# Sharing the last product of a decode-attention kernel with GpSimd, with smaller last pieces behind it

## The chip, the core and the metric

The kernel runs on one core of a Trainium2 chip. Time is device time in microseconds (us), taken as the median of several executions; less is better. A core has TensorE (matrix products, PE in the rows), VectorE (DVE), ScalarE (ACT), GpSimd (POOL) and SyncE (SP, which here only issues loads). Each has its own instruction queue and they meet at semaphores. Sixteen DMA engines move data between HBM and the on-chip SBUF, whose 128 partitions are the rows of every tile; TensorE writes to PSUM.

## What is computed

One token for each of two sequences goes through cached attention with 16 heads, 4096 keys and a head size of 256, and through a small dense layer with a squared ReLU. A gate mixes the two.

```python
q = (x @ wq)                                   # 2 x 16 heads x 256
scores = einsum("bhqd,bhkd->bhqk", q, k_cache) * 256 ** -0.5
o = einsum("bhqk,bhkd->bhqd", softmax(scores), v_cache)
a = o.reshape(B, 1, 4096) @ wo
h = x @ w1 + b1;  b = relu(h) ** 2 @ w2 + b2
g = sigmoid((x * gate_w).sum(-1))
out = g * a + (1 - g) * b                      # 2 x 1 x 448, all float32
```

Each of the two caches has 134 MB, and with the weights 289.6 MB go through the core once.

## The kernel before

The two caches are read in 16 rounds. A round takes two heads `t` of one sequence `b`: 8 MB of keys and 8 MB of values. Keys and values lie with 64 of a head's 4096 keys in each partition (64 partitions for each of the two heads), so one partition holds 64 x 256 = 16384 numbers of each.

A round `r` runs through the engines like this:

- VectorE multiplies the whole key tile by q in place (line 213, the q of the head spread over 64 keys), which waits for the keys' landing; then it takes the reciprocal and the small product `rl` of the round before (`normed`, lines 198 and 199), sums each key's 256 products into `s` (line 222), and takes the maximum over the partition's 64 keys (`m`, line 223).
- TensorE spreads the maxima (`mt`), VectorE takes their maximum, negated (`nb`, line 224), ScalarE makes the exponentials `p` in two halves with their sums (line 240), and TensorE adds these sums over the partitions (`sm`).
- TensorE multiplies values by `p`: 32 matmuls into `po`, each written as two records in the profile since the numbers are float32. ScalarE copies `po` to `o` (line 193), TensorE turns it with `rl` as the scale (`ot`), and ScalarE copies the result into `oT` (line 194).

The loads stand in SyncE's queue in the order in which they are written, and each waits there for what frees its tile: keys of round r + 2 for the sums of round r, values of round r for TensorE's values of round r - 1. There are two key tiles and one value tile. The last values go into a free key tile instead, in two pieces cut at `V_CUT` keys, once the sums of round 14 are done. The output weights wo go into the value tile behind the values of round 14, in five pieces, cut after 16, 24, 28, 31 and 32 blocks (`WO_CUTS`).

After the last round comes the output projection: 32 blocks of 128 rows of wo. All but the last `LATE` are added into `acc`, with two rows of output and 448 columns; all matmul lines appear as line 265, a helper. The late ones are added into `fin`, 112 columns at a time in four parts of the array, from `wide`, into which VectorE has copied their part of `oT` (line 258). ScalarE copies `acc` to `ya` (line 260), and a matmul with `pick` adds it into `fin` in the middle of the late blocks. VectorE copies the result (`y`, line 261) and SyncE stores it.

```python
for i, (t, k) in enumerate(blocks):
    if i == WO_CUTS[i_w]:
        pe.wait_ge(WL[i_w].h, 16)
        i_w += 1
    ...
    if n == LATE // 2:
        pe.wait_ge(AC.h, AC_YA)
        late(pick, ya)
    ins = late(wide[:, n, :], rhs, n == 0, n == LATE - 1)
```

The name of a tile is given in the rows without its number: `k` is either key tile, `v` the value tile.

Of the kernel before, what the change touches and what calls it, by code (L numbers as in the profile page):

```python
# [7 lines left out]
ALU = mybir.AluOpType  # L8
AX = mybir.AxisListType

P = 128
WO_ORDER = [0, 1, 2, 3, 7, 4, 5, 6]
LATE = 8
WO_CUTS = (0, 16, 24, 28, 31, 32)
V_CUT = 48


class Count:
# [16 lines left out]
def gated_mix_kernel(nc, b2, wq, wf, wo, k_cache, v_cache, out):  # L35
    B, H, S, DH = k_cache.shape
# [5 lines left out]
    KEYS = 2 * S // P  # L42
# [11 lines left out]
    pe, dve, act, pool, sp = nc.tensor, nc.vector, nc.scalar, nc.gpsimd, nc.sync  # L54
    rounds = [(t, b) for t in range(T) for b in range(B)]
    R = len(rounds)

    def sb(name, *free):
        return nc.alloc_sbuf_tensor(name, [P, *free], F32)[:]
# [12 lines left out]
    pick = sb("pick", W)  # L72
    wide = sb("wide", LATE, W)
    p8 = sb("p", NM, 4)
    s = sb("s", KEYS)
# [18 lines left out]
    DV, AC, TE, GP = (Count(nc, n) for n in ("dve", "act", "pe", "pool"))  # L94
    KL = [Count(nc, "k0_landed"), Count(nc, "k1_landed")]
# [14 lines left out]
    def kv(cache, r):  # L110
        t, b = rounds[r]
        return cache[b, 2 * t:2 * t + 2].rearrange("h (p j) d -> (h p) (j d)", j=KEYS)

    def load(dst, src, sem, after=None):
        ins = sp.dma_start(dst, src)
        if after:
            after[0].on(ins, after[1])
        return sem.up(ins, 16)
# [10 lines left out]
    def te_mt(r):  # L129
        return TE_MT0 if r == 0 else TE_SUM0 + 4 * (r - 1) + 3  # L130
# [4 lines left out]
    def te_val(r):  # L135
        return TE_SUM0 + 4 * r + 1

    def te_ot(r):
        return TE_SUM0 + 4 * r + 2

    TE_ACC = te_ot(R - 1) + 1
    TE_FIN = TE_ACC + 1


    pool.memset(ident, 0.0)
    GP.up(pool.memset(ones, 1.0))
# [37 lines left out]
    AC_QB = [AC.up(TE.on(act.activation(qb[:, i, :], QBANK[i % 4], AF.Copy), TE_QB[i])) for i in range(T * B // 2)]  # L184
# [6 lines left out]
    def turned(r):  # L191
        t, b = rounds[r]
        OC.up(TE.on(act.activation(o, po, AF.Copy), te_val(r)))  # L193
        AC_OT[r] = AC.up(TE.on(act.activation(oT[:, t, :, b, :], ot[:, :NJ * 2].rearrange("p (j h) -> p j h", h=2), AF.Copy), te_ot(r)))  # L194

    def normed(r):
        b = rounds[r][1]
        n = DV.up(TE.on(dve.reciprocal(rc, sm[:, :2]), te_sum(r)))
        RL.up(DV.on(dve.scalar_tensor_tensor(rl, rc.unsqueeze(1).to_broadcast([P, 2, 2]), gP[:, 0, b:b + 1],
                                             sel.rearrange("p (s h) -> p s h", s=2), op0=ALU.mult, op1=ALU.mult), n))  # L200

    def k_view(r):
        return keys[r % 2].rearrange("p (j d) -> p j d", d=DH)

    load(keys[1], kv(k_cache, 1), KL[1], (TE, TE_Q1))
    for r, (t, b) in enumerate(rounds):
        kt = k_view(r)
        q = qb[:, (t // 2) * B + b, (t % 2) * DH:(t % 2 + 1) * DH]
        if r < 4:
            dve.wait_ge(AC.h, AC_QB[(t // 2) * B + b])  # L210
        elif r == 4:
            dve.wait_ge(AC.h, AC_QB[-1])
        n = DV.up(KL[r % 2].on(dve.tensor_tensor(kt, kt, q.unsqueeze(1).to_broadcast([P, KEYS, DH]), op=ALU.mult), 16 * (r // 2 + 1)))  # L213
        if r == 0:
            DV_H = DV.up(TE.on(dve.tensor_tensor(hb, sm[:, :FC * B].rearrange("p (c b) -> p c b", b=B), b1T.unsqueeze(2).to_broadcast([P, FC, B]), op=ALU.add), TE_PT))
            DV_H = DV.up(DV.on(dve.tensor_scalar(hb, hb, 0.0, None, op0=ALU.max), DV_H))
            DV_H = DV.up(DV.on(dve.tensor_mul(hT, hb, hb), DV_H))
            DV_H = DV.up(DV.on(dve.tensor_tensor(hT, hT, gP[:, 1, :].unsqueeze(1).to_broadcast([P, FC, B]), op=ALU.mult), DV_H))
            load(vals, kv(v_cache, 0), VL, (TE, TE_ADD))
        else:  # L220
            normed(r - 1)
        DV_S = DV.up(DV.on(dve.tensor_reduce(s, kt, axis=AX.X, op=ALU.add), n))  # L222
        MX.up(DV.on(dve.tensor_reduce(m, s, axis=AX.X, op=ALU.max), DV_S))
        DV_NB = DV.up(TE.on(dve.tensor_reduce(nb, mt[:, :64], axis=AX.X, op=ALU.max, negate=True), te_mt(r)))  # L224
        if r > 0:
            turned(r - 1)
            if r < R - 1:
                load(vals, kv(v_cache, r), VL, (TE, te_val(r - 1)))
            else:
                for i, (lo, hi) in enumerate(zip(WO_CUTS, WO_CUTS[1:])):  # L230
                    load(vals[:, lo * D:hi * D], wo[:, lo * D:hi * D], WL[i], (TE, te_val(r - 1)) if i == 0 else None)
        if r + 2 < R:
            load(keys[r % 2], kv(k_cache, r + 2), KL[r % 2], (DV, DV_S))
        elif r + 2 == R:
            at = V_CUT * DH
            load(keys[r % 2][:, :at], kv(v_cache, R - 1)[:, :at], VT[0], (DV, DV_S))
            load(keys[r % 2][:, at:], kv(v_cache, R - 1)[:, at:], VT[1])
        for hh in range(2):
            z = slice(64 * hh, 64 * hh + 64)
            e = act.activation(p8[z, :, hh:hh + 3:2], s[z].rearrange("p (m s) -> p m s", s=2), AF.Exp,  # L240
                               bias=nb[z], accum_out=rsm[z, hh:hh + 1])
            if hh == 0:
                DV.on(e, DV_NB)
            else:
                EX.up(e)
# [3 lines left out]
    blocks = [(t, k) for t in WO_ORDER for k in range(4)]  # L249
    early = len(blocks) - LATE  # L250

# [21 lines left out]
    def done(ins, n):  # L273
        ins.then_inc(TE.h, 1)
        te[0] += 1
        assert te[0] == n, (te[0], n)

    def values(v, lo=0, hi=NM):
        vv = v.rearrange("p (m s d) -> p m (s d)", s=2, d=DH)
        for i in range(lo, hi):  # L280
            g = 32 * (i % 4)
            ins = mm(po[g:g + 4, :], p8[:, i, :], vv[:, i, :], i < 4, i >= NM - 4)
        return ins

    def turn():
        take(OC)
        take(RL)
        for j in range(NJ):
            for x in range(2):
                at = x * DH + j * P  # L290
                ins = mm(ot[:, j * 2:j * 2 + 2], o[:, at:at + P], rl[:, x, :], x == 0, x == 1)
        return ins
# [11 lines left out]

    n_acc = 1 + FC + T * 4 - LATE
    added = [0]
# [7 lines left out]
    def late(lt, rhs, start=False, stop=False):  # L314
        for k in range(4):
            ins = mm(fin[32 * k:32 * k + W, :DQ], lt, rhs[:, k * DQ:(k + 1) * DQ], start, stop)
        return ins
# [59 lines left out]
    pe.wait_ge(VT[0].h, 16)  # L377
    values(keys[R % 2], 0, V_CUT // 2)
    pe.wait_ge(VT[1].h, 16)
    done(values(keys[R % 2], V_CUT // 2, NM), te_val(R - 1))  # L380
    done(turn(), te_ot(R - 1))
    pe.wait_ge(AC.h, AC_OT[R - 1])
    i_w = 0
    for i, (t, k) in enumerate(blocks):
# [9 lines left out]
        n = i - early  # L394
        if n == 0:
            pe.wait_ge(DV.h, DV_W)
# [4 lines that stand above are left out]
    done(ins, TE_FIN)  # L401
# [74 lines left out]
```

## Time and profile before

| what | value |
|---|---|
| median of 3 runs | 677.21 us (676.92 to 678.72) |
| the profiled execution's own time | 678.37 us |
| its span | 676.2 us |
| mean granted TensorE clock | 0.641 |
| VectorE busy | 566.5 us, 84% |
| TensorE busy | 219.1 us, 32% |
| GpSimd busy | 2.1 us, all in the first 3 us |
| moved by DMA | 289.63 MB, mean 428 GB/s |

The span goes from the first to the last recorded instruction of the execution; the execution's own time is 2.2 us longer. In the rows a group has its source line, its engine, the operation, the tile written and the tile read, with partitions x elements; a bracket at the end of a row tells how long the engine had been idle and which engine or transfer released it. The clock is the share of full speed that TensorE was granted.

### The profile page before, as it was taken

The numbers are of one execution on the slowest core, as the hardware profiler recorded it, in microseconds if no ns is written. First come the engines' busy times: TensorE is split into PE (matmuls) and PEld (weight loads), VectorE is DVE, ScalarE is ACT, GpSimd is POOL, SyncE is SP. The second block draws the span as 40 slices with busy tenths as digits, with TensorE's granted clock in tenths as the row PEclk, the third lists the DMA queues.
The fourth block names the chain that finished last, engine by engine and source line by source line (L and its number), as shares of the span: only waits on it lengthen the run. The fifth ranks groups of instructions, "written<-read, shape, count | busy, mean of one in ns | idle before, by whom it ended". The sixth has DMA issues, their size and how long they took to land. (4 is left out here: it accounts for less than half of the span.)

```text
span 676.2 us, 3474 instructions
## 1 busy us (share of the span) xinstructions
PE 219.1 (32%) x1522; PEld 68.1 (10%) x1522; DVE 566.5 (84%) x120; ACT 36.1 (5%) x111; POOL 2.1 (0%) x15
## 2 busy tenths in 40 slices
PE   0726142140605123060603206060512406050368
PEld 0211001010101101010100101010010101010022
DVE  1067999999979797998979798997979799897950
ACT  0121000000000000000000000000000000000000
POOL 1000000000000000000000000000000000000000
PEclk9976656585756557575755757575665758575568
DMA  9999999999999999999999999999999999999996
GB/s 381 438 445 421 434 435 434 434 434 434 434 435 434 430 434 431 434 434 434 434 434 434 434 434 434 434 434 434 434 434 434 434 434 434 434 434 434 418 423 284
DMA packets 5779, 289.63 MB, mean 428 GB/s; under 512 B 653, under 2 KB 782, under 8 KB 1038
## 3 DMA queue, kind: packets, MB, share of 16 engines
q1 hardware_dynamic: 5772, 289.56, 99.1%
q8 instruction: 3, 0.05, 0.0%
q14 instruction: 2, 0.02, 0.0%
q10 hardware_dynamic: 2, 0.00, 0.0%
HBM read 289.55 MB, written 0.00 MB: 428 GB/s over the span
## 5 line engine op out<-in xcount | busy, mean ns | idle before, releaser
L213 DVE TENSOR_TENSOR k<-k,q 128x16384 f32<-128x16384 f32 x16 | 275.6, 17224 | 52.7 <-DMA k<-in_k_cache_dram 52.7
L222 DVE TENSOR_REDUCE s<-k 128x64 f32<-128x16384 f32 x16 | 275.4, 17212 | 0.0
L265 PE MATMUL po<-v,p 128*4 128x512 f32 x960 | 138.1, 740 | 295.1 <-PEq L269 295.1
L265 PEld LDWEIGHTS po<-v,p 128*4 128x4 f32 x960 | 26.6, 99 | 394.0 <-issue 394.0
L265 PE MATMUL mt<-ident,m 128*64 128x64 f32 x64 | 7.7, 334 | 84.1 <-PEq L269 84.1
L193 ACT ACTIVATE o<-po 128x512 f32<-128x512 f32 x16 | 9.6, 597 | 454.9 <-PE po L265 454.9
L265 PE MATMUL ot<-rl,o 128*128 128x2 f32 x128 | 16.4, 250 | 15.6 <-PEq L269 15.6
L265 PEld LDWEIGHTS ot<-rl,o 128*128 128x128 f32 x128 | 15.5, 191 | 30.0 <-issue 30.0
L240 ACT ACTIVATE p<-s,nb 64x64 f32<-64x64 f32 x32 | 11.2, 350 | 101.4 <-DVE nb L224 101.2
L265 PE MATMUL sm<-rsm,ones 128*128 128x2 f32 x32 | 8.9, 348 | 21.2 <-PEq L269 21.2
L174 DVE COPY pk<-k 128x28 f32<-128x28 f32 x1 | 0.2, 180 | 16.5 <-DMA k<-in_wq_dram 16.5
L265 PEld LDWEIGHTS mt<-ident,m 128*64 128x64 f32 x64 | 5.2, 205 | 85.8 <-issue 85.8
L224 DVE TENSOR_REDUCE nb<-mt 128x1 f32<-128x64 f32 x16 | 3.6, 224 | 10.7 <-PE mt L265 10.7
L265 PEld LDWEIGHTS sm<-rsm,ones 128*128 128x128 f32 x32 | 8.0, 311 | 23.8 <-issue 23.8
L265 PE MATMUL fin<-v,pk 128*2 128x448 f32 x32 | 5.0, 785 | 15.9 <-DMA v<-in_wf_dram 15.9
L265 PE MATMUL pq<-k,pk 128*2 128x512 f32 x64 | 9.9, 789 | 0.0
L258 DVE COPY wide<-oT 128x2 f32<-128x2 f32 x8 | 0.7, 162 | 11.0 <-ACT oT L194 11.0
L265 PE MATMUL po<-k,p 128*4 128x512 f32 x64 | 9.3, 745 | 0.0
L265 PE MATMUL sm<-ys,ones 128*128 128x2 f32 x2 | 0.6, 349 | 21.0 <-DVE ys L177 21.0
L261 DVE COPY y<-fin 128x112 f32<-128x112 f32 x1 | 0.3, 275 | 7.6 <-PE fin L265 7.6
L265 PE MATMUL acc<-v,oT 128*2 128x448 f32 x48 | 6.3, 686 | 0.3 <-ACT oT L194 0.3
L240 ACT ACTIVATION_READ_ACCUMULATOR p<-s,nb 64x1 f32 x32 | 5.9, 185 | 0.0
(59 smaller groups left out, 60.1 us busy)
## 6 DMA issues: line engine op xcount, KB each, us to landing
k<-in_wq_dram SPq DMA_DIRECT2D x1, 7182.0 KB, 19.5
v<-in_wf_dram SPq DMA_DIRECT2D x1, 6272.0 KB, 52.8
k<-in_v_cache_dram SPq DMA_DIRECT2D x1, 6144.0 KB, 37.8
v<-in_wo_dram SPq DMA_DIRECT2D x1, 3584.0 KB, 18.0
k<-in_v_cache_dram SPq DMA_DIRECT2D x1, 2048.0 KB, 42.4
v<-in_wo_dram SPq DMA_DIRECT2D x1, 1792.0 KB, 22.0
v<-in_wo_dram SPq DMA_DIRECT2D x1, 896.0 KB, 23.7
v<-in_wo_dram SPq DMA_DIRECT2D x1, 672.0 KB, 24.8
```

Source lines behind the costliest of these rows:

```text
L174: DV_PK = DV.up(QL.on(dve.tensor_copy(pk, keys[1][:, 3 * N + N // 2:3 * N + N // 2 + PK]), 16))
L193: OC.up(TE.on(act.activation(o, po, AF.Copy), te_val(r)))
L213: n = DV.up(KL[r % 2].on(dve.tensor_tensor(kt, kt, q.unsqueeze(1).to_broadcast([P, KEYS, DH]), op=ALU.mult), 16 * (r // 2 + 1)))
L222: DV_S = DV.up(DV.on(dve.tensor_reduce(s, kt, axis=AX.X, op=ALU.add), n))
L224: DV_NB = DV.up(TE.on(dve.tensor_reduce(nb, mt[:, :64], axis=AX.X, op=ALU.max, negate=True), te_mt(r)))
L240: e = act.activation(p8[z, :, hh:hh + 3:2], s[z].rearrange("p (m s) -> p m s", s=2), AF.Exp, bias=nb[z], accum_out=rsm[z, hh:hh + 1])
L258: DV_W = dve.tensor_copy(wide[:, n, 0:W:16], o_block(t, k))
L261: DV_Y4 = DV.up(TE.on(dve.tensor_copy(y4, fin[:, :DQ]), TE_FIN))
L265: return pe.matmul(dst, lt, rhs, start=start, stop=stop)
```

## The change

In the last round alone, VectorE multiplies only the first 48 of 64 keys by q, and GpSimd the other 16 (`HELP`); both wait for the landing of the keys, GpSimd also for the last q. VectorE sums the 48 keys, waits for GpSimd, and sums the 16. The last values' two pieces are 40 and 24 keys instead of 48 and 16. Four blocks instead of eight are late. Ahead of VectorE's and ScalarE's programs stands a directive that places what follows at a multiple of 128 instruction slots, the gap being jumped over.

```diff
-LATE = 8
+LATE = 4
 WO_CUTS = (0, 16, 24, 28, 31, 32)
-V_CUT = 48
+V_CUT = 40
+HELP = 16
...
+    for e in (dve, act):
+        e.addr_align(128, 0, max_nops=0)
...
-        n = DV.up(KL[r % 2].on(dve.tensor_tensor(kt, kt, q.unsqueeze(1).to_broadcast([P, KEYS, DH]), op=ALU.mult), 16 * (r // 2 + 1)))
+        own = KEYS if r < R - 1 else KEYS - HELP
+
+        def times_q(e, lo, hi):
+            return KL[r % 2].on(e.tensor_tensor(kt[:, lo:hi], kt[:, lo:hi], q.unsqueeze(1).to_broadcast([P, hi - lo, DH]), op=ALU.mult), 16 * (r // 2 + 1))
+
+        n = DV.up(times_q(dve, 0, own))
+        if own < KEYS:
+            pool.wait_ge(AC.h, AC_QB[-1])
+            GP_HELP = GP.up(times_q(pool, own, KEYS))
...
-        DV_S = DV.up(DV.on(dve.tensor_reduce(s, kt, axis=AX.X, op=ALU.add), n))
+        DV_S = DV.up(DV.on(dve.tensor_reduce(s[:, :own], kt[:, :own], axis=AX.X, op=ALU.add), n))
+        if own < KEYS:
+            DV_S = DV.up(GP.on(dve.tensor_reduce(s[:, own:], kt[:, own:], axis=AX.X, op=ALU.add), GP_HELP))
```

VectorE's program in the last round, before (`k` is the key tile, `s` the sums, the words in brackets the semaphores that an instruction waits for):

```order
L213 TENSOR_TENSOR k<-k,q 128x16384 [waits k1_landed]
L198 RECIPROCAL rc<-sm 128x2 [waits pe]
L199 SCALAR_TENSOR_TENSOR rl<-rc,gP,sel 128x4 [waits dve]
L222 TENSOR_REDUCE s<-k 128x64 [waits dve]
L223 TENSOR_REDUCE m<-s 128x1 [waits dve]
```

And now, with new line numbers:

```order
L220 TENSOR_TENSOR k<-k,q 128x12288 [waits k1_landed]
L202 RECIPROCAL rc<-sm 128x2 [waits pe]
L203 SCALAR_TENSOR_TENSOR rl<-rc,gP,sel 128x4 [waits dve]
L234 TENSOR_REDUCE s<-k 128x48 [waits dve]
L236 TENSOR_REDUCE s<-k 128x16 [waits pool]
L237 TENSOR_REDUCE m<-s 128x1 [waits dve]
```

The product and the sums lose 16 keys, and a second sum that waits for GpSimd stands ahead of the maximum. On TensorE the end of the program before, from the last values on (`v_tail0` and `v_tail1` are the pieces of the values, `wo0` to `wo4` those of wo):

```order
L265 MATMUL po<-k,p 4x512 x23
L265 MATMUL po<-k,p 4x512 [waits v_tail1]
...
L265 MATMUL acc<-v,oT 2x448 [waits wo1_landed]
L265 MATMUL acc<-v,oT 2x448 x7
L265 MATMUL fin<-v,wide 17x112 [waits dve,wo2_landed]
L265 MATMUL fin<-v,wide 17x112 x15
L265 MATMUL fin<-ya,pick 17x112 [waits act,wo3_landed]
```

And now:

```order
L279 MATMUL po<-k,p 4x512 x19
L279 MATMUL po<-k,p 4x512 [waits v_tail1]
...
L279 MATMUL acc<-v,oT 2x448 [waits wo2_landed]
L279 MATMUL acc<-v,oT 2x448 x3
L279 MATMUL fin<-v,wide 17x112 [waits dve,wo3_landed]
L279 MATMUL fin<-v,wide 17x112 x7
L279 MATMUL fin<-ya,pick 17x112 [waits act]
```

The wait for the second piece of values moved from the 25th to the 21st matmul, and the third piece of wo now goes into `acc`, so that the late blocks begin with the fourth.

## The prediction

> **What bounds the kernel now.** I read the page first: how busy each engine is and what the transfers move.
>
> ```profile
> span 676.2 us, 3474 instructions
> PE 219.1 (32%) x1522; PEld 68.1 (10%) x1522; DVE 566.5 (84%) x120; ACT 36.1 (5%) x111; POOL 2.1 (0%) x15
> GB/s 381 438 445 421 434 435 434 434 434 434 434 435 434 430 434 431 434 434 434 434 434 434 434 434 434 434 434 434 434 434 434 434 434 434 434 434 434 418 423 284
> q1 hardware_dynamic: 5772, 289.56, 99.1%
> ```
>
> The queue of loads is busy for 99.1% of the span, and in the slices the rate stands at 430 to 435 GB/s from the fifth to the last three. VectorE's 84% is cover, not bound. So a change can win only after the last bytes land, or by making them land earlier. Next came the timeline of the last round, in order of time (start, length, engine, what):
>
> ```profile
> 616.94 17.23 DVE L213 TENSOR_TENSOR k<-k,q 128x16384 f32<-128x16384 f32 x1 [2.87 <-DMA k<-in_k_cache_dram]
> 634.08 0.16 DVE L198 RECIPROCAL rc<-sm 128x2 f32<-128x2 f32 x1
> 634.28 0.22 DVE L199 SCALAR_TENSOR_TENSOR rl<-rc,gP,sel 128x4 f32<-128x4 f32 x1
> 634.42 17.21 DVE L222 TENSOR_REDUCE s<-k 128x64 f32<-128x16384 f32 x1
> 651.67 0.22 DVE L223 TENSOR_REDUCE m<-s 128x1 f32<-128x64 f32 x1
> ...
> 654.33 9.28 PE L265 MATMUL po<-k,p 128*4 128x512 f32 x64
> ...
> 663.69 0.60 ACT L193 ACTIVATE o<-po 128x512 f32<-128x512 f32 x1 [9.99 <-PE po L265]
> 664.59 1.02 PE L265 MATMUL ot<-rl,o 128*128 128x2 f32 x8 [0.97 <-PEq L269]
> 665.65 0.17 ACT L194 ACTIVATE oT<-ot 128x4 f32<-128x4 f32 x1 [1.36 <-PE ot L265]
> 665.88 6.28 PE L265 MATMUL acc<-v,oT 128*2 128x448 f32 x48 [0.26 <-ACT oT L194]
> 671.98 0.94 PE L265 MATMUL fin<-v,wide 128*17 128x112 f32 x32
> 672.23 0.54 ACT L260 ACTIVATE ya<-acc 128x448 f32<-128x448 f32 x1 [6.41 <-PE acc L265]
> 673.11 0.96 PE L265 MATMUL fin<-v,wide 128*17 128x112 f32 x32
> 674.13 0.28 DVE L261 COPY y<-fin 128x112 f32<-128x112 f32 x1 [7.62 <-PE fin L265]
> ```
>
> Here is a chain without a gap: the product, the sums and the maximum on VectorE, the exponentials, then TensorE (values, turn, 48 records of the output projection, the late blocks) up to 674.07. The last transfers run beside it. Their issue times and their times to landing (KB, then us from issue) are:
>
> ```profile
> 612.96 0.80 SPq L115 DMA_DIRECT2D k<-in_v_cache_dram  x2
> 646.18 2.23 SPq L115 DMA_DIRECT2D v<-in_wo_dram  x5
> L115 SPq DMA_DIRECT2D v<-in_wo_dram x5: 328/432/433, 646.2 to 648.0; - x5
> k<-in_v_cache_dram SPq DMA_DIRECT2D x1, 6144.0 KB, 37.8
> k<-in_v_cache_dram SPq DMA_DIRECT2D x1, 2048.0 KB, 42.4
> v<-in_wo_dram SPq DMA_DIRECT2D x1, 3584.0 KB, 18.0
> v<-in_wo_dram SPq DMA_DIRECT2D x1, 1792.0 KB, 22.0
> v<-in_wo_dram SPq DMA_DIRECT2D x1, 896.0 KB, 23.7
> v<-in_wo_dram SPq DMA_DIRECT2D x1, 672.0 KB, 24.8
> v<-in_wo_dram SPq DMA_DIRECT2D x1, 224.0 KB, 24.8
> ```
>
> Issue plus time to landing gives 650.8 and 655.8 (the second issued at 613.4) for the two pieces of values. The five of wo were issued 0.45 apart, so they land at 664.2, 668.6, 670.8, 672.3 and 672.8. TensorE starts on the first wo piece at 665.88, 1.7 after it landed, and ends at 674.07, 1.3 after the last landing. Both chains end close together: this is what limits the gain.
>
> **The change, step by step.** None of the last loads waits for anything that moves: the values wait for the sums of round 14, wo for the values of round 14 (the five issues from 646.18). The landings above stay.
>
> *Product and sums.* VectorE multiplies 48 of 64 keys: 17.23 x 0.75 = 12.92, from 616.94 to 629.86, 4.31 less. The sums of all 64 keys stay on VectorE as 48 and 16 keys; the second instruction adds about 0.15, by the maximum over 64 elements that takes 0.22. So s is ready 4.15 earlier: 48 keys summed at 643.1, 16 more at 647.5.
>
> *GpSimd's share*, 4096 elements per partition with two inputs. No row shows such an operation; these are the nearest, with those that cover the start:
>
> ```profile
> 0.87 0.10 POOL L146 MEMSET ones<- 128x1 f32 x1
> 1.40 1.00 POOL L153 COPY v<-ident 128x128 f32<-128x128 f32 x4
> 20.31 0.18 DVE L174 COPY pk<-k 128x28 f32<-128x28 f32 x1 [16.48 <-DMA k<-in_wq_dram]
> 21.63 0.17 ACT L178 ACTIVATE gP<-sm 128x2 f32<-128x2 f32 x1 [19.07 <-PE sm L265]
> ```
>
> A copy of 128 elements takes 0.25, 0.15 above the one-element memset: 1.2 ns an element, 4.8 us for 4096 as the low end. The whole 0.25 per 128 elements, doubled for two inputs, gives 16.0 as the high end. I take 9.6, the slope doubled, because the copy is the same engine reading SBUF and only the second input is new. Begun with VectorE's product it ends at 626.5, and even at 16.0 at 632.9: well ahead of 643.1, where the sums of the 16 keys ask for it. If it is held until VectorE's product ends, it ends at 639.5, still in time. Of the two waits that come with it, GpSimd's has only the clearing of semaphores at the end behind it, and VectorE's has the sums of 16 keys, the maximum and with it all of the chain. VectorE may itself lose between nothing and the whole of GpSimd's time to the shared work; I take nothing, since nothing in these rows makes VectorE wait for GpSimd, and price the other end below.
>
> *Values as 40 and 24 keys.* The first piece loses 1024 of 6144 KB; 2048 KB lie 5.0 us apart in the landings, so it lands 2.5 earlier, at 648.3. TensorE can start at 654.33 - 4.15 = 650.2, after it; with the old cut it would have waited until 650.8. Its pace, and the clock granted (0.50 is half speed), are in these stages (stage, length, PE busy and count, ..., clock, DMA share, GB/s):
>
> ```profile
> 654.30:658.90 4.60, 4.60 (x25) 0.86 (x29) 0.40 (x2) 0.00 (x0) 0.00 (x0) 0.50 1.08 462
> 658.90:663.60 4.70, 4.70 (x44) 0.87 (x36) 0.00 (x0) 0.00 (x0) 0.00 (x0) 1.00 0.92 388
> 665.80:669.30 3.50, 3.42 (x20) 0.70 (x24) 0.66 (x8) 0.02 (x1) 0.00 (x0) 0.53 0.97 402
> 669.30:672.00 2.70, 2.70 (x36) 0.70 (x32) 0.00 (x0) 0.00 (x0) 0.00 (x0) 1.00 0.64 257
> 672.00:674.10 2.10, 2.07 (x76) 1.59 (x68) 0.00 (x0) 0.54 (x1) 0.00 (x0) 1.00 0.03 10
> ```
>
> At this pace (some 22 records in the 4.6 cold us, then 0.107 each) the 40 records of the first piece end at 656.7, after the second has landed at 655.8: no wait. The values end near 659.5 and oT is ready near 661.7, 4.15 ahead of 665.88.
>
> *What is late next.* The first wo piece lands at 664.2: TensorE waits 2.5, and of the 4.15 only 1.7 is left. After this wait I take the same cold stretch as after 665.8, 20 records in 3.42; later ones are 0.10 each (28 in the 2.86 that remain of the 6.28). Blocks 0 to 15 (32 records) end at 664.2 + 3.42 + 1.2 = 668.8, blocks 16 to 23 at 670.4; the next piece lands at 670.8.
>
> *Four late blocks.* Eight records of 0.10 join acc (+0.8), 32 of 0.029 leave fin (-0.94), and four of VectorE's eight copies to wide go, beside TensorE's work. Blocks 24 to 27 end at 671.6 and ya is copied by 672.25, needed about 0.47 after the next landing, at 672.8. That landing is 672.3. Behind it stand two late blocks, ya and two more: 40 records, 1.2 us, to 673.5. The last landing, 672.8, comes before its block's turn. Against 674.07 this is 0.5 us earlier; y and the output follow unchanged.
>
> *Aligned programs.* VectorE and ScalarE get a jump at the start. No row shows what it costs. Up to about 16 us it is hidden by the idle 16.48 ahead of VectorE's first copy from a load and the 19.07 ahead of ScalarE's first result; without that cover it would be added to the first q, and so to the first product. A gain is bounded by the same rows at nothing, since both engines are waiting there anyway. I take nothing.
>
> Sum: 676.2 - 0.5 = 675.7 of span. The profiled execution took 678.37, 2.2 more than its span and 1.2 above the median; from the median 677.21 the forecast is 676.7.
>
> **Rivals.**
>
> *GpSimd and VectorE exclude each other.* Both instructions become ready with the same landing, and both read k and q from SBUF. If one of them waits for the other, the order does not save VectorE: with GpSimd first, the product starts late by GpSimd's whole time; with VectorE first, GpSimd runs from 629.9, and the small two-input operation on rl (634.28 now, between product and sums) waits for it, with the sums behind it. So VectorE loses 9.6 against a gain of 4.15: all of TensorE's tail, which then meets landed data and takes its 8.2 us as before, is 5.4 later: 682.6. Up to 2.5 of loss is hidden by the wait at 664.2; it is slower than before from 4.15, and by 0.3% from 6.2. At 4.8 it would be +0.6, 677.8. For it speaks that nowhere in this trace do the two engines read SBUF at once, so no row denies it; against it, that VectorE's rows show no wait on GpSimd. [...]
>
> *TensorE's clock stays at half.* If the new waits (2.5, 0.4, 0.7) keep the clock at 0.50 after 664.2, records cost 0.171 and 0.058: blocks 0 to 27 end at 664.2 + 56 x 0.171 = 673.8, the 40 last at 676.1, 2.0 later than now: 679.2. Against it: the clock was back at 1.00 after 3.5 us of work at 669.3, and the waits after that are short.
>
> *The gain is hidden, or the floor is met.* If VectorE loses between 2.5 and 4.15, the time is 676.7 to 677.2. If TensorE keeps up with the last landing, one block (8 x 0.029) follows 672.8: 1.0 less, 676.2.
>
> **How the numbers follow.** 0.3% is 2.0 us, about what a measurement of this kernel can tell from no change. Forecast 0.62 (own range 676.0 to 677.7, with the spread of the three runs); hidden or floor 0.13; exclusion 0.17, of which 0.02 ends within 0.3%; clock 0.03, of which 0.01 within; an earlier landing or start that I cannot see, over 0.3%, 0.04; a start that is not covered 0.01. Same: 0.62 + 0.13 + 0.02 + 0.01 = 0.78; slower 0.15 + 0.02 + 0.01 = 0.18; faster 0.04. The range 675.6 to 680.2 leaves out the exclusion's main part and the far faster case, just under 0.2.
>
> **What would show it.** Right: VectorE's product of 12.9 from the landing near 617, the 48-key sums at once behind rl, values from 650 without a stop, TensorE idle before the first wo block until 664.2, and the chain that ended last beginning at a landing of wo with 1.2 us of fin behind it. Wrong: a product longer than 13, a gap ahead of rl or of the sums, GpSimd's end after 643, a clock of 0.5 beyond 668, or loads issued at other times than now.

## The result: 0.55% slower

The changed kernel takes 681.0 us (median of 8 runs) against 677.04 us: a ratio of 1.0055 with a 95% interval of 1.004 to 1.0069. The forecast was 676.7, the same within 0.3%. Two executions far above all others, of 1218.69 us without GpSimd's share and 748.19 us of an unaligned kernel below, are left out of the ratios. The profiled execution took 682.67 us with a span of 681.2, 5.0 longer than in the trace before; the medians differ by 4.0. Its page:

```profile
span 681.2 us, 3426 instructions
PE 220.0 (32%) x1498; PEld 67.7 (10%) x1498; DVE 570.3 (84%) x117; ACT 36.1 (5%) x111; POOL 23.6 (3%) x16
q1 hardware_dynamic: 5772, 289.56, 98.4%
```

VectorE has lost a quarter of one product and is yet 3.8 us busier (566.5 before). The last round in the timeline of the changed kernel says where:

```profile
617.17 12.96 DVE L220 TENSOR_TENSOR k<-k,q 128x12288 f32<-128x12288 f32 x1 [2.87 <-DMA k<-in_k_cache_dram]
617.22 21.58 POOL L220 TENSOR_TENSOR k<-k,q 128x4096 f32<-128x4096 f32 x1 [614.50 <-DMA k<-in_k_cache_dram]
630.04 0.16 DVE L202 RECIPROCAL rc<-sm 128x2 f32<-128x2 f32 x1
630.24 8.58 DVE L203 SCALAR_TENSOR_TENSOR rl<-rc,gP,sel 128x4 f32<-128x4 f32 x1
638.74 12.94 DVE L234 TENSOR_REDUCE s<-k 128x48 f32<-128x12288 f32 x1
651.61 4.40 DVE L236 TENSOR_REDUCE s<-k 128x16 f32<-128x4096 f32 x1
656.04 0.22 DVE L237 TENSOR_REDUCE m<-s 128x1 f32<-128x64 f32 x1
...
658.71 9.55 PE L279 MATMUL po<-k,p 128*4 128x512 f32 x64
668.33 0.60 ACT L197 ACTIVATE o<-po 128x512 f32<-128x512 f32 x1 [10.26 <-PE po L279]
...
670.52 7.14 PE L279 MATMUL acc<-v,oT 128*2 128x448 f32 x56 [0.26 <-ACT oT L198]
677.48 0.57 PE L279 MATMUL fin<-v,wide 128*17 128x112 f32 x16
677.73 0.54 ACT L274 ACTIVATE ya<-acc 128x448 f32<-128x448 f32 x1 [7.26 <-PE acc L279]
678.32 0.39 PE L279 MATMUL fin<-ya,pick 128*17 128x112 f32 x8 [0.28 <-ACT ya L274]
678.53 0.57 PE L279 MATMUL fin<-v,wide 128*17 128x112 f32 x16
```

The row to read is rl: four numbers per partition, 0.22 us before, 8.58 us now. It stands still from the end of the product to 638.82, and GpSimd's row ends at 638.80. GpSimd's own length of 21.58 holds 12.9 of waiting, if what comes behind VectorE's product is its work: the product ends at 630.13, and 8.67 are left (experiments below bear this out). No row is marked as a wait: it lies within the busy row, and only the length, 8.58 for 0.22, betrays it.

From keys' landing to maximum VectorE now takes 38.87 us (617.17 to 656.04) instead of 34.73, 4.14 more: the product saves 4.27, rl adds 8.36, the sums in two pieces 0.13, less a little overlap. Beside it 0.23 come from a later landing of the keys, 0.26 from the values' matmuls (9.55 for 9.28), 0.39 from the projection and the late blocks. Together 5.02: the end of fin went from 674.07 to 679.10.

The transfers, issue rows and times to landing:

```profile
613.18 0.80 SPq L116 DMA_DIRECT2D k<-in_v_cache_dram  x2
645.35 2.23 SPq L116 DMA_DIRECT2D v<-in_wo_dram  x5
k<-in_v_cache_dram SPq DMA_DIRECT2D x1, 5120.0 KB, 35.4
v<-in_wo_dram SPq DMA_DIRECT2D x1, 3584.0 KB, 19.1
v<-in_wo_dram SPq DMA_DIRECT2D x1, 224.0 KB, 26.0
```

The first values land at 648.6, the first wo at 664.5 and the last near 673.1, within 0.4 us of the forecast's landings, though wo was issued 0.8 earlier than before. TensorE reaches wo at 670.52 and waits for none of it: the kernel went from nearly transfer bound at its end to VectorE bound there.

### The profile page after: what moved, and what is told of

It is laid out like the page before. It is cut to its first block, busy times and chain, and to the rows that moved or that the text cites. A ratio compares the mean times of both kernels' runs of the same rounds, so it can differ in the third digit from the quotient of the medians.

```text
span 681.2 us, 3426 instructions
## 1 busy us (share of the span) xinstructions
PE 220.0 (32%) x1498; PEld 67.7 (10%) x1498; DVE 570.3 (84%) x117; ACT 36.1 (5%) x111; POOL 23.6 (3%) x16
## 5 line engine op out<-in xcount | busy, mean ns | idle before, releaser
L220 DVE TENSOR_TENSOR k<-k,q 128x16384 f32<-128x16384 f32 (+1 forms) x16 | 271.3, 16957 | 52.0 <-DMA k<-in_k_cache_dram 52.0
L234 DVE TENSOR_REDUCE s<-k 128x64 f32<-128x16384 f32 (+1 forms) x16 | 271.1, 16945 | 0.0
L220 POOL TENSOR_TENSOR k<-k,q 128x4096 f32<-128x4096 f32 x1 | 21.6, 21582 | 614.5 <-DMA k<-in_k_cache_dram 614.5
L203 DVE SCALAR_TENSOR_TENSOR rl<-rc,gP,sel 128x4 f32<-128x4 f32 x16 | 11.9, 745 | 0.6
```

The costliest lines, as they stand in the source:

```text
L220: return KL[r % 2].on(e.tensor_tensor(kt[:, lo:hi], kt[:, lo:hi], q.unsqueeze(1).to_broadcast([P, hi - lo, DH]), op=ALU.mult), 16 * (r // ...
L234: DV_S = DV.up(DV.on(dve.tensor_reduce(s[:, :own], kt[:, :own], axis=AX.X, op=ALU.add), n))
```

## Experiments

The theory, drawn from the 8.58 us of rl, which ended with GpSimd: an instruction of VectorE with two tensors from SBUF as inputs and GpSimd's product, which reads SBUF, exclude each other, whole. The rivals: GpSimd holds whatever VectorE does next; or the loss is in another part of the change.

### rl ahead of the last product

```diff
+        if own < KEYS:
+            normed(r - 1)
         n = DV.up(times_q(dve, 0, own))
...
-        else:
+        elif own == KEYS:
             normed(r - 1)
```

> The changed kernel with one move: in the last round VectorE makes the reciprocal and rl ahead of its product instead of behind it. Theory (two SBUF inputs): only an instruction that reads two SBUF tensors waits for GpSimd, so rl takes its usual 0.22 us near 616, GpSimd is held until the product ends near 630 and then runs some 8.6 us beside the 48-key sums, which take 12.94 us and start at once. s is ready near 647.7, the values start near 650.4, TensorE waits for the first piece of wo, and the time is 676.5 us, 0.5 under the kernel before. Rival (GpSimd's reads hold whatever VectorE does next): the sums start near 638.7 in place of rl, and the time stays at 681 us.

Measured: 677.13 us, ratio 0.9991 (0.9983 to 1.0), 0.6 over the 676.5 that was expected. Its timeline:

```profile
616.49 0.22 DVE L203 SCALAR_TENSOR_TENSOR rl<-rc,gP,sel 128x4 f32<-128x4 f32 x1
617.49 12.96 DVE L220 TENSOR_TENSOR k<-k,q 128x12288 f32<-128x12288 f32 x1 [0.78 <-DMA k<-in_k_cache_dram]
617.54 21.62 POOL L220 TENSOR_TENSOR k<-k,q 128x4096 f32<-128x4096 f32 x1 [614.81 <-DMA k<-in_k_cache_dram]
630.49 12.95 DVE L236 TENSOR_REDUCE s<-k 128x48 f32<-128x12288 f32 x1
643.36 4.41 DVE L238 TENSOR_REDUCE s<-k 128x16 f32<-128x4096 f32 x1
...
664.86 8.07 PE L281 MATMUL acc<-v,oT 128*2 128x448 f32 x56 [2.06 <-DMA v<-in_wo_dram]
```

The 48-key sums, with one input, run beside GpSimd's 8.7 us at their own pace: 12.95 us, for 12.94 in the changed kernel, where GpSimd had ended. The rival that GpSimd holds whatever comes next falls. The last row has what the forecast expected of the change itself: TensorE waits 2.06 us for the first wo.

### rc in PSUM, the order as in the change

```diff
-    rc = sb("rc", 2)
...
+    rc = sm[:, 64:66]
```

> The changed kernel with the reciprocal rc kept in PSUM instead of SBUF, in all rounds, the order unchanged: the operation on rl then has one SBUF tensor as input and one from PSUM. Theory (two SBUF inputs): rl is not held, takes 0.2 to 0.3 us behind the product, and the time is 676.5 us. Rival (the place in the program or the write decides, not the number of SBUF inputs): rl takes some 8.6 us again, 681 us.

Measured: 677.27 us, ratio 0.9996 (0.9987 to 1.0005).

```profile
617.03 21.61 POOL L220 TENSOR_TENSOR k<-k,q 128x4096 f32<-128x4096 f32 x1 [614.30 <-DMA k<-in_k_cache_dram]
629.85 0.17 DVE L202 RECIPROCAL sm<-sm 128x2 f32<-128x2 f32 x1
630.06 0.22 DVE L203 SCALAR_TENSOR_TENSOR rl<-sm,gP,sel 128x4 f32<-128x4 f32 x1
...
664.38 7.33 PE L279 MATMUL acc<-v,oT 128*2 128x448 f32 x56 [3.84 <-DMA v<-in_wo_dram]
```

Same place, same write into SBUF, one input moved to PSUM: 0.22 us for 8.58. With a second tensor from SBUF rl waited, without one it did not. TensorE again waits for the first wo, here 3.84 us. The time is 0.8 over what was expected and cannot be told from no change.

### Without GpSimd's share

```diff
-HELP = 16
+HELP = 0
```

> The changed kernel without GpSimd's share (HELP = 0): 40 and 24 keys, four late blocks and the aligned programs alone. Theory: these parts cost nothing that can be measured, 677.0 us as before, within 0.3%; at most 0.4 us more, since with four late blocks TensorE waits 0.28 us for ya. Rival (the tail with four late blocks, the other cut or the jump cost what was lost): 680 to 681 us.

Measured: 677.18 us, ratio 0.9998 (0.9989 to 1.0007). The cut of 40, the four late blocks and the aligned programs together cost nothing that can be measured.

### GpSimd's share alone, on the kernel before

```diff
-LATE = 4
+LATE = 8
-V_CUT = 40
+V_CUT = 48
-    for e in (dve, act):
-        e.addr_align(128, 0, max_nops=0)
```

> The kernel before with GpSimd's share of 16 keys as the only change: values as 48 and 16 keys, eight late blocks, programs not aligned. Theory: rl is held for 8.6 us and the time is that of the changed kernel, 681 us, less up to 0.4 us, since with eight late blocks TensorE does not wait for ya. Rival (the loss needs one of the other parts): 677 us.

Measured: 680.97 us, ratio 1.0055 (1.0037 to 1.0072), the ratio of the whole change. rl again:

```profile
629.86 8.57 DVE L200 SCALAR_TENSOR_TENSOR rl<-rc,gP,sel 128x4 f32<-128x4 f32 x1
```

### 8 keys instead of 16

```diff
-HELP = 16
+HELP = 8
```

> The changed kernel with 8 keys on GpSimd instead of 16. Theory (rl waits for GpSimd's whole time): GpSimd works 4.3 us behind a product of 15.1 us, rl ends near 636.7, s is ready near 654.0, 2.3 us later than in the kernel before: 679 us. Rival (a fixed cost of sharing, whatever the size): 681 us or more, since VectorE saves less.

Measured: 679.33 us, ratio 1.0023 (1.0011 to 1.0035).

```profile
617.55 19.39 POOL L220 TENSOR_TENSOR k<-k,q 128x2048 f32<-128x2048 f32 x1 [614.84 <-DMA k<-in_k_cache_dram]
632.71 4.25 DVE L203 SCALAR_TENSOR_TENSOR rl<-rc,gP,sel 128x4 f32<-128x4 f32 x1
```

rl follows GpSimd's work: 8.58 against 4.25 for 2048 elements more, 2.1 ns an element. The two sizes leave no fixed cost that shows.

### Which of the two goes first

Three kernels try to let GpSimd begin before VectorE's product. First, a one-element memset of a scratch tile that waits for the landing:

```diff
+        if own < KEYS:
+            DV.up(KL[r % 2].on(dve.memset(scr, 0.0), 16 * (r // 2 + 1)))
         n = DV.up(times_q(dve, 0, own))
```

> The changed kernel with a small memset on VectorE ahead of the last product; the memset waits for the keys' landing, so that VectorE reaches its product some 0.1 us after GpSimd has begun. Theory (the two exclude each other, whoever starts first goes first): GpSimd runs from 617.2 for 8.6 us to about 625.8, VectorE's product ends near 638.8 instead of 630.1, rl then takes its 0.22 us, s is ready near 656, and the time is that of the changed kernel, 681 us. Rival (VectorE always goes ahead of GpSimd): the product takes 12.96 us and rl is held again for 8.6 us; the time is 681 us too, so the rows decide. Rival (no exclusion between the two products, only rl is slow): product 12.96 us, GpSimd done by 626, rl 0.22 us, 676.5 to 677 us.

Measured: 680.43 us, ratio 1.0045 (1.0029 to 1.0061). The product's row still began 0.04 ahead of GpSimd's (617.06 and 617.10), and rl was held for 8.57 us again, so this one doesn't tell. Then 448 elements, over `ya`, which is still free then:

```diff
-            DV.up(KL[r % 2].on(dve.memset(scr, 0.0), 16 * (r // 2 + 1)))
+            DV.up(KL[r % 2].on(dve.memset(ya, 0.0), 16 * (r // 2 + 1)))
```

> The changed kernel with a memset of 448 elements (some 0.47 us) on VectorE ahead of the last product; it waits for the keys' landing, so that GpSimd begins 0.4 us ahead of the product. Theory (whichever of the two begins first holds the other): GpSimd ends 8.6 us after its start, near 625.8, VectorE's product starts or ends 8.6 us late (end near 638.8), rl takes 0.22 us, and the time is that of the changed kernel, 681 us. Rival (the product goes ahead of GpSimd in any order): the product takes 12.96 us from 617.6, GpSimd ends near 639.2 and rl is held: 681 us too, so the rows decide. Rival (no exclusion between the two products): both run from 617 at their own pace and the time is 676.5 to 677.5 us.

Measured: 680.45 us, ratio 1.0052 (1.0036 to 1.0067).

```profile
616.85 21.99 POOL L220 TENSOR_TENSOR k<-k,q 128x4096 f32<-128x4096 f32 x1 [614.13 <-DMA k<-in_k_cache_dram]
616.92 0.43 DVE L223 MEMSET ya<- 128x448 f32 x1 [2.98 <-DMA k<-in_k_cache_dram]
617.27 12.89 DVE L220 TENSOR_TENSOR k<-k,q 128x12288 f32<-128x12288 f32 x1
630.27 8.59 DVE L203 SCALAR_TENSOR_TENSOR rl<-rc,gP,sel 128x4 f32<-128x4 f32 x1
```

GpSimd's row leads by 0.42, and still the product went ahead of it, at full pace. This spoke for the rival that VectorE always passes. So the last, with seven such memsets, each waiting for the one ahead:

```diff
+            n = DV.up(KL[r % 2].on(dve.memset(ya, 0.0), 16 * (r // 2 + 1)))
+            for _ in range(6):
+                n = DV.up(DV.on(dve.memset(ya, 0.0), n))
```

> The changed kernel with seven memsets of 448 elements, one behind the other, on VectorE between the keys' landing and its product (some 3.3 us in all), so that GpSimd has 3 us of its 8.6 behind it when the product is ready to start. Theory (an instruction that has begun holds the other until it ends): VectorE's product shows 12.96 us and what is left of GpSimd's work, some 5 to 6 us, as idle time or as length: it ends near 638.7, GpSimd near 625.8, and rl takes 0.22 us; the time is 681 us. Rival (VectorE's product is never held, and GpSimd stops when it comes): the product takes 12.9 us from 620.2, GpSimd ends some 5.6 us after it, near 638.7, and rl is held for those 5.6 us: 681 us. Both give the same time; the rows of the product and of rl decide.

Measured: 682.43 us, ratio 1.0045 (1.0008 to 1.0081).

```profile
617.04 8.82 POOL L220 TENSOR_TENSOR k<-k,q 128x4096 f32<-128x4096 f32 x1 [614.32 <-DMA k<-in_k_cache_dram]
621.02 17.66 DVE L220 TENSOR_TENSOR k<-k,q 128x12288 f32<-128x12288 f32 x1
638.79 0.22 DVE L203 SCALAR_TENSOR_TENSOR rl<-rc,gP,sel 128x4 f32<-128x4 f32 x1
```

Now GpSimd runs undisturbed, 8.82 to 625.86, and the product is longer by 4.7: from 625.86 to its end at 638.68 it has 12.82, about the 12.96 that it takes elsewhere. rl is short, 0.22. So in these traces whichever had really begun held the other to its end; the order with GpSimd ahead was seen in this one trace. In either order VectorE ends some 8.6 us late: here 3.9 went by in the memsets and 4.7 in the longer product. How long after the start of its row GpSimd takes hold lies, by these two traces, between 0.42 us and 4.0; it wasn't narrowed down.

### In search of a faster version

With rl out of the way the end hangs on wo's landing, and three orders of the tail were tried on the kernel with rl ahead. Eight late blocks, with ya added before the wait for the fourth piece:

```diff
-LATE = 4
+LATE = 8
...
+        if i - early == LATE // 2:
+            pe.wait_ge(AC.h, AC_YA)
+            late(pick, ya)
         if i == WO_CUTS[i_w]:
...
-        if n == LATE // 2:
-            pe.wait_ge(AC.h, AC_YA)
-            late(pick, ya)
```

> The changed kernel with rl ahead of the last product, eight late blocks, and ya added before TensorE waits for the fourth piece of wo instead of behind it. Theory: the end is set by the landing of the last pieces of wo; behind the fourth piece 32 records of 0.029 us are left instead of 40, so the time is 0.2 us under that of the kernel with rl ahead alone, 676.9 us, and 0.3 to 0.6 us under the kernel before. Rival (TensorE's tail still sets the end): 677.1 us or more.

Measured: 677.93 us, ratio 1.0004 (0.9995 to 1.0014): a miss. In its trace fin ends 1.0 us earlier than in that of rl ahead alone, whose acc kept half the pace for longer (four weight loads in 0.75 us instead of 0.37, until about 670.0; here until 667.4), and only 0.2 earlier than with rc in PSUM; and the store took longer. SyncE's wait at the end and a DMA queue that the profile marks as instruction (its packets come first), first of this kernel, then of the same one without the aligned programs:

```profile
SPq L426 <- SPq L426: 1.8, 1, 1.8
q14 instruction: 3, 0.02, 0.0%
```

```diff
-    for e in (dve, act):
-        e.addr_align(128, 0, max_nops=0)
```

> The kernel with rl ahead, eight late blocks and ya added ahead of the wait (677.9 us, with a store of the output that took 0.8 us longer and one more fetch on an instruction queue), without the aligned programs. Theory (that fetch falls into the store since the aligned VectorE program with eight copies just passes a block's end): queue q14 fetches twice as before, the store takes 1.0 us again, and the time is 676.9 to 677.1 us. Rival (the eight late blocks or the order at the end cost it): 677.9 us again.

```profile
SPq L423 <- SPq L423: 1.0, 1, 1.0
q14 instruction: 2, 0.02, 0.0%
```

Measured: 677.02 us, ratio 0.9997 (0.9987 to 1.0006). Unaligned, the third packet of that queue is gone and the store takes 1.0 again. That fetching it held the store is likely, but not shown: only the alignment was varied, and no trace shows a block of instructions whose end the program passed. For it speaks that in all seven other traces where both were read (before, the change, rl ahead, rc in PSUM, GpSimd's share alone, 448 elements, ya first) the queue had 2 packets and the store took 1.0. Last, four late blocks, aligned, with ya first of all in fin:

```diff
+        if i == early:
+            pe.wait_ge(AC.h, AC_YA)
+            late(pick, ya, True)
         if i == WO_CUTS[i_w]:
...
-        if n == LATE // 2:
-            pe.wait_ge(AC.h, AC_YA)
-            late(pick, ya)
```

> The changed kernel with rl ahead of the last product, and ya added into fin ahead of the late blocks and of the wait for the fourth piece of wo; four late blocks, aligned. Theory (the end is set by wo's last landings): 32 instead of 40 records follow the fourth landing, 0.2 us less than with rl ahead alone: 676.8 to 677.0 us, 0.2 to 0.6 us under the kernel before. Rival (the tail has no such slack, since the output projection ends after that landing): 677.1 us as with rl ahead alone.

Measured: 677.23 us, ratio 1.0005 (0.9996 to 1.0014): no gain.

```profile
655.66 2.76 PE L281 MATMUL po<-k,p 128*4 128x512 f32 x24 [1.69 <-DMA k<-in_v_cache_dram]
...
672.27 0.39 PE L281 MATMUL fin<-ya,pick 128*17 128x112 f32 x8 [0.66 <-ACT ya L276]
```

Now it is ya that TensorE waits for, and the four late blocks start no earlier than wo's fourth landing would let them. No version was found that beats the kernel before by more than can be measured.

## Why the prediction was wrong

- **The step that failed** is GpSimd's share: "VectorE may itself lose between nothing and the whole of GpSimd's time to the shared work; I take nothing, since nothing in these rows makes VectorE wait for GpSimd." It lost 8.4 us, the length that rl gained (8.58 for 0.22). The rows could not show such a wait: before the change GpSimd does nothing after the first 3 us. Absence from a trace in which the case never arises is no evidence for either end.
- **The rival had the mechanism**, and even the instruction: with VectorE first, rl waits for GpSimd with the sums behind it. Its chance of 0.17 was the error. Its time, 682.6, was 1.6 too high. GpSimd's work was put at 9.6 and takes 8.6 to 8.8, which is 0.9 of that. The rest is probably the clock of the last section: the sum kept 8.2 us for a tail that had begun at a clock of 0.53.
- Which instructions wait, and for whom, the runs show for this kernel: rl with two SBUF inputs was held (8.58), with one it was not (0.22, rc in PSUM), nor were the sums (12.95), and the order of starting decided who was held (the product, by 4.7, when GpSimd was 4 us ahead).
- **Product and sums** were right: 12.96 for 12.92, 48 keys in 12.94, 16 more in 4.40.
- **Values as 40 and 24 keys**: the first piece landed at 648.6, for 648.3. With TensorE at 658.71 it did not matter. That TensorE would not wait for the second piece was forecast for a clock that starts at half, and at half it did start in the changed kernel (0.50 from 658.7 to 662.4). With ya first, the first 40 records took 4.47 us, 0.11 each, the pace that the trace before has at 1.00, and TensorE waited 1.69 (the row above), hidden by the longer wait for wo.
- **What is late next** was right as a mechanism, once rl was moved: a wait for the first wo of 2.06 and 3.84 us (2.5 forecast). The forecast of 0.5 less is what those kernels show at best (0.9991 and 0.9996), within what can be told from no change. Its base flattered it: the 0.5 came from the trace of an execution of 678.37 us and was taken off a median of 677.21. Beside rl ahead (677.01 to 677.96) the kernel before took 676.69 to 679.08 in 35 runs, so some of its executions already ended as early.
- **Four late blocks**: the forecast set 0.8 us more in acc against 0.94 less in fin, and had no wait for ya. Where TensorE is the late one, as here, ya comes 0.28 late, and from the start of acc the tail takes 8.58 for 8.19. Without GpSimd's share it takes 8.58 too, which is lost in the 0.9998.
- **Aligned programs**: the later start was covered as forecast. VectorE began 0.57 later and ScalarE's table load 2.37 later (0.92 and 1.28 before), and both still waited for the first load:

```profile
1.49 1.03 DVE L165 MEMSET pq<- 128x512 f32 x2 [1.49 <-PEq L476]
3.65 1.28 ACT L182 ACT_TABLE_LOAD   x1 [3.65 <-issue]
20.77 0.18 DVE L178 COPY pk<-k 128x28 f32<-128x28 f32 x1 [16.38 <-DMA k<-in_wq_dram]
22.09 0.17 ACT L182 ACTIVATE gP<-sm 128x2 f32<-128x2 f32 x1 [17.15 <-PE sm L279]
```

But that copy itself began 0.46 later than before (20.31), since the load landed later, and the forecast had no term for this. The landing is later in all nine traces with aligned programs where it was read (19.9 to 20.2 us from issue) than in the three without (19.5 to 19.6). In the last round it no longer shows: VectorE takes up the keys at 616.86 to 617.50 with, at 616.79 to 617.19 without. The alignment alone was not run.

- The second rival, a clock that stays at half, did not come about in the changed kernel, which has none of the new waits that it needs. With rl ahead, which has them, it came in part: in that trace four weight loads of acc came in 0.75 us from its start, 664.86, until about 670.0, that is for 5.1 us where 3.4 were forecast, and in 0.37 after that. In the trace before these are the paces at a clock of 0.50 (666 to 669) and of 1.00 (from 670). acc took 8.07 us (7.33 with rc in PSUM). That execution, of 677.96 us, was the slowest of its eleven.

## What to carry to other kernels

Before work is handed to GpSimd, list what VectorE does while it runs. In these runs an instruction with two tensors from SBUF, even one of four numbers per partition, waited for all that was left of GpSimd's product (8.58 us with 16 keys, 4.25 with 8), and all behind it in VectorE's queue waited too. Put such instructions ahead, or give them an operand in PSUM (0.22 us either way), and let sums over one tensor run beside GpSimd (12.95 us, for 12.94 when GpSimd was done). Only one kind of GpSimd instruction was tried here, a product that reads SBUF. And where the transfers end 1.3 us before the kernel does, as in the trace before, 4 us saved ahead of them are worth 1.3 at the most: compute that ceiling before anything else.

## What was not expected of the hardware

The runs of the changed kernel lie in two groups, 679.55 to 679.99 and 682.01 to 682.69, four of eight in each, which is why the median stands between them. The traces point to a cause within TensorE. The same 56 records of acc (28 matmuls; every matmul here is float32 and shows as two records, so no run tells whether the type is why), after the same short pause, took 7.14 us in the changed kernel, in an execution of the upper group, and 5.44 with the one-element memset (its time 680.43). They differ in the granted clock. The stage in the changed kernel, then acc and its stage in the other:

```profile
670.50:674.00 3.50, 3.48 (x20) 0.78 (x24) 0.38 (x4) 0.00 (x0) 0.00 (x0) 0.52 0.26 103
```

```profile
669.93 5.44 PE L282 MATMUL acc<-v,oT 128*2 128x448 f32 x56 [0.26 <-ACT oT L199]
669.90:675.30 5.40, 5.37 (x62) 1.59 (x66) 0.38 (x4) 0.00 (x0) 0.00 (x0) 1.00 0.23 90
```

A clock of 0.52 against 1.00 over the first 3.5 us goes with 1.70 us, and the values' matmuls took 0.47 more (9.55 for 9.08): together 2.17 of the 2.24 us between these two executions. Two more traces with rl or the product held, with the memset of 448 elements (680.35 us) and with seven of them (682.89), agree:

```profile
669.69 5.44 PE L281 MATMUL acc<-v,oT 128*2 128x448 f32 x56 [0.26 <-ACT oT L198]
670.73 7.14 PE L283 MATMUL acc<-v,oT 128*2 128x448 f32 x56 [0.27 <-ACT oT L198]
```

With 8 keys acc took 7.14 too, in the slowest of its twelve executions (681.22). What makes the clock drop in one execution and not in another stays open, since each kernel left one trace. So here a tail that TensorE bounds carried an uncertainty of this size from run to run: the changed kernel's eight runs spread over 3.14 us. Where TensorE waits for wo anyway the spread was smaller: 0.95 us in eleven runs with rl ahead, 1.39 with rc in PSUM, 1.20 with ya first.
